# Batch 0 of a fused attention and maxout-MoE kernel in two query parts, with its loads reordered

## Chip, cores, metric

One Trainium2 chip, one core. The metric is the device time of one launch in microseconds, the median of several runs. The profile of the kernel before is of one further run; that of every other kernel is of the first of its runs. PE is TensorE, DVE VectorE, ACT ScalarE, POOL GpSimd, SP SyncE. Every run told here is of the state "fast". Within that state some runs have a mean granted TensorE clock of 0.99 instead of 1.0, and where it matters I give them apart.

## The reference

```python
# q, k, v: (8 batches, 8 heads, 576 rows, 64)
scores = scale * q @ k.T                 # per batch and head
scores = where(block_i >= block_j, scores, -1e9)   # causal in blocks of 64
attn   = exp(scores - max); attn /= attn.sum(-1) + 1e-9
x = (attn @ v)  -> (4608 tokens, 512)
h1, h2 = x @ w1, x @ w2                  # 512 -> 1024
out = maximum(h1, h2) @ w_out            # 1024 -> 512
```

## The kernel before

Heads are handled in pairs (32 pairs, four to a batch; two pairs make a group whose q and k are loaded together). For a pair, PE makes transposed scores (keys on partitions), ACT takes the exp into `aT`, POOL zeroes the half blocks above the diagonal, PE multiplies with V ("AV"; V has a column of ones, so the row sums come along), DVE divides, and PE transposes the result into `xT` ("x_out"), from which the MoE takes 512 tokens at a time ("a span"): h products against w1 and w2, the maximum on DVE, y products against w_out. The MoE's products are dealt out between the attention's by `fill(n)`. q and k are loaded as they are ("plain loads", issued by SP and ACT) and cast to bf16 by an engine; V and the weights are cast on the way ("casting loads", issued by POOL). Feature block f is h's columns 128f to 128f + 127, so block 4 is the first that needs weights from column 512 on, the last to be loaded. The opening of the kernel before:

```python
load_qk(0, (SP, ACT)); load_qk(1, (SP, SP)); load_qk(2, (SP, SP))
# ... casts of groups 0 and 1, V of batch 0, then:
load_w(0, 256); load_w(256, 256)         # on POOL's queue, cast to bf16 on the way

warm_up(16)                              # products of zeros, for the clock
# ... transposes of group 0 ...
for s in range(HP):                      # HP = 4: the pairs of batch 0
    burst_a(s)                           # scores and exps of 1024 + 1024 elements
    # ... casts, transposes, warm_up, av(0, ...) by s ...
    burst_b(s)                           # 1024 + 128
    pool_work(s)                         # s == 0: load_w(512, 512); load_qk(3); s == 3: load_qk(4), V1, w_out
for p in (1, 2, 3):
    av(p, [0, 1]); av(p, [2, 3, 4])      # query tiles of 128 rows
    if p == 2:
        x_out(0)
x_out(1)                                 # only now is a token ready for the MoE
for s in range(HP, NPAIR):               # the even rhythm, with fill() between
    burst_a(s); fill(n_a); burst_b(s); pool_work(s); av(s - 2, ...); ...
```

The softmax here doesn't subtract the row's maximum and nothing guards it: scores larger than these inputs give would overflow.

## Time and profile before

| | before |
|---|---|
| time, median of 4 runs | 294.64 us (293.98 to 294.97) |
| PE busy in the profiled run | 281.2 of 292.3 us |
| of which products of zeros | 36, 10.7 us |
| first useful MoE product | 27.1 us |
| pair 4's first scores (the even rhythm begins) | 32.04 us |
| end of the last product | 289.06 us |

Read it like this: PE is the engine that is full, so the time is PE's list of work plus the stretches in which it does not do useful work.

### The profile page before, as it was taken

The page shows a single profiled execution, that of the slowest core. Times are in us where ns is not written, and L with a number is a line of the kernel's source. Part 1 is how long each engine was busy: PE and PEld are TensorE (multiplying, and loading weights), DVE is VectorE, ACT ScalarE, POOL GpSimd, SP SyncE. Part 2 cuts the span into 40 slices and gives each one's busy share as a digit, 9 for nine tenths or more (in the row PEclk, how much of TensorE's full clock was granted, in tenths as well). Part 3 has the DMA queues.
Part 4 walks back from the last instruction along what each step waited for, and adds up shares of the span by engine and source line. Part 5 has one row for each costly group of instructions (what it writes and reads, how often), then busy time and mean ns, then how long its engine had stood idle before and what let it go on. Part 6 is the DMA issues. An engine that isn't in the chain of part 4 may idle for free.

```text
span 292.3 us, 7455 instructions
## 1 busy us (share of the span) xinstructions
PE 281.2 (96%) x3116; PEld 141.0 (48%) x3116; DVE 181.9 (62%) x363; ACT 140.2 (48%) x200; POOL 95.7 (33%) x236
## 2 busy tenths in 40 slices
PE   8787999999999999999999999999999999999995
PEld 3345445445554454544454455454545544444443
DVE  6717677547986676666565656666665766464530
ACT  3883686686655555554545555545555000101112
POOL 2967536625644443144324532443111000000000
PEclk9999999999999999999999999999999999999999
DMA  7999999968923792568656594465110111011104
GB/s 265 288 182 295 224 183 172 234 150 166 200 34 142 97 212 46 199 73 201 82 200 72 116 168 153 76 61 65 40 38 37 38 69 41 36 72 38 72 36 144
DMA packets 56081, 36.65 MB, mean 125 GB/s; under 512 B 38768, under 2 KB 43376, under 8 KB 56048
## 3 DMA queue, kind: packets, MB, share of 16 engines
q0 software_dynamic: 41728, 7.87, 34.5%
q1 hardware_dynamic: 13760, 27.60, 27.8%
q10 hardware_dynamic: 560, 0.72, 0.7%
q8 instruction: 24, 0.39, 0.6%
q14 instruction: 9, 0.07, 0.1%
HBM read 34.60 MB, written 9.44 MB: 151 GB/s over the span
## 4 chain that ended last, share of the span: by engine, by line
PE 89%; ACT 4%; DVE 3%; DMA 2%; issue 1%; ACTq 0%
PE ps_h L168 43%; PE ps_y L186 20%; PE ps_o L333 11%; PE ps_s L282 8%; ACT aT L288 3%; PE ps_qT L265 2%; DMA qraw<-in_q_dram 2%; PE ps_kT L265 2%; PE ps_xe L353 2%; PE ps_w L254 1%; DVE xp L340 1%; PE ps_y L203 1%; DVE xT L358 0%; DVE qT L272 0%; DVE kT L272 0%
## 5 line engine op out<-in xcount | busy, mean ns | idle before, releaser
L168 PE MATMUL ps_h<-xT,w_sb 128*128 128x512 bf16 x576 | 139.6, 380 | 0.5 <-DVE xT L359 0.4
L288 ACT ACTIVATE aT<-ps_s 128x1024 bf16<-128x1024 f32 (+1 forms) x128 | 99.2, 832 | 53.5 <-PE ps_s L282 53.5
L168 PEld LDWEIGHTS <-w_sb 128*128 128x128 bf16 x576 | 51.8, 98 | 59.7 <-issue 6.1
L175 DVE CAST h<-ps_h 128x512 bf16<-128x512 f32 x72 | 49.7, 691 | 45.0 <-PE ps_h L168 43.9
L186 PE MATMUL ps_y<-wo_sb,g 128*128 128x512 bf16 x280 | 69.6, 379 | 0.0
L293 POOL MEMSET aT<- 64x128 bf16 x128 | 23.6, 200 | 120.7 <-ACT aT L288 120.5
L192 ACT COPY y<-ps_y 128x512 f32<-128x512 f32 x35 | 20.5, 587 | 83.9 <-PE ps_y L186 61.4
L177 DVE TENSOR_TENSOR g<-h,ps_h 128x512 bf16<-128x512 bf16 x72 | 49.3, 684 | 10.2 <-PE ps_h L168 10.2
L333 PEld LDWEIGHTS <-aT 128*128 128x128 bf16 x960 | 33.6, 98 | 14.9 <-DVE xp L340 8.4
L333 PE MATMUL ps_o<-vv,aT 128*128 128x65 bf16 x960 | 39.7, 194 | 0.9 <-DVE xp L340 0.4
L186 PEld LDWEIGHTS <-g 128*128 128x128 bf16 x280 | 25.4, 98 | 27.9 <-issue 3.2
L282 PE MATMUL ps_s<-qT,kT 64*128 64x64 bf16 (+4 forms) x384 | 34.5, 275 | 3.0 <-ACT aT L288 2.9
L109 POOL DMA_DIRECT2D vv<-in_v_dram x40 | 33.7, 848 | 0.3 <-issue 0.3
L340 DVE TENSOR_TENSOR xp<-ps_o,rec 128x256 bf16<-128x256 f32 x64 | 31.4, 491 | 2.2
L282 PEld LDWEIGHTS <-kT 64*128 64x128 bf16 x384 | 16.5, 94 | 18.9 <-issue 13.2
L339 DVE RECIPROCAL rec<-ps_o 128x4 f32<-128x4 f32 x64 | 11.8, 184 | 18.9 <-PE ps_o L333 18.8
L105 POOL CAST qn<-qraw 128x1152 bf16<-128x1152 f32 (+1 forms) x15 | 17.1, 1138 | 4.8 <-DMA qraw<-in_q_dram 4.7
L272 DVE COPY qT<-ps_qT 128x576 bf16<-128x576 bf16 x17 | 12.8, 757 | 5.3 <-PE ps_qT L265 4.1
L358 DVE COPY xT<-ps_xe 128x640 bf16<-128x640 bf16 x16 | 7.8, 490 | 12.4 <-PE ps_xe L353 12.1
L105 POOL CAST kn<-kraw 128x1152 bf16<-128x1152 f32 x13 | 14.9, 1145 | 1.9 <-DMA kraw<-in_k_dram 1.2
L272 DVE COPY kT<-ps_kT 128x576 bf16<-128x576 bf16 x17 | 12.8, 756 | 4.3 <-PE ps_kT L265 3.3
L254 PE MATMUL ps_w<-zeros 128*128 128x512 bf16 x36 | 10.7, 432 | 1.7 <-DVE zeros L132 1.2
(39 smaller groups left out, 102.9 us busy)
## 6 DMA issues: line engine op xcount, KB each, us to landing
qraw<-in_q_dram SPq DMA_DIRECT2D x16, 576.0 KB, 4.4
out_dram<-y SPq DMA_DIRECT2D x35, 256.0 KB, 2.1
kraw<-in_k_dram SPq DMA_DIRECT2D x15, 576.0 KB, 6.5
vv<-in_v_dram POOLq DMA_DIRECT2D x32, 128.0 KB, 5.8
w_sb<-in_moe_w_dram POOLq DMA_DIRECT2D x4, 256.0 KB, 8.1
w_sb<-in_moe_w_dram POOLq DMA_DIRECT2D x2, 512.0 KB, 16.9
wo_sb<-in_moe_w_out_dram POOLq DMA_DIRECT2D x2, 512.0 KB, 12.6
kraw<-in_k_dram ACTq DMA_DIRECT2D x1, 576.0 KB, 5.6
```

Source lines behind the costliest of these rows:

```text
L105: copy(out=n[:, j0:j1], in_=t[:, j0:j1])
L109: nc.gpsimd.dma_start(out=vv_r[b % NV][:rows, c, :, :D], in_=v[b, :, c * P:c * P + rows, :].rearrange("h p d -> p h d"),)
L168: nc.tensor.matmul(pt[:], w_sb[:, c, f * P:(f + 1) * P], xT[:, c, t0:t0 + SPAN], start=(c == 0), stop=(c == NDM - 1),)
L175: nc.vector.tensor_copy(out=h1[:], in_=pt[:])
L177: nc.vector.tensor_max(g[:, f, :], h1[:], pt[:])
L186: nc.tensor.matmul(py[:], g[:, f, s * P:(s + 1) * P], wo_sb[:, f, :], start=(f == 0), stop=(f == NFF - 1),)
L272: copies[i](out=t[:, :S].rearrange("q (p j) -> q p j", j=RPP), in_=pts[i].rearrange("q j p -> q p j"),)
L282: nc.tensor.matmul(ps[:m, hh, col:col + w], kT[r, c * P:c * P + m], qT[r, q0:q0 + w], start=True, stop=True,)
L288: nc.scalar.activation(out=aT_r[p % NA][:m, :, a0:a0 + w], in_=ps[:m, :, :w], func=AF.Exp, scale=scale,)
L293: nc.gpsimd.memset(aT_r[p % NA][BLK:, :, a0:a0 + BLK], 0.0)
L333: nc.tensor.matmul(po[:, gi, hh, :], a[:, hh, a0:a0 + P], vv[:, c, h0 + 2 * hh, :], start=(mm == 0), stop=(mm == n_mm - 1),)
L340: nc.vector.tensor_mul(xp[:, ts[0]:ts[0] + n, :, p % 2], po[:, :, :, :D], rec[:, :n].to_broadcast([P, n, 2, D]),)
```

## The change

The intent: start the MoE earlier. Batch 0 is done in two query parts, queries 0 to 255 of all four pairs first, so that 256 tokens are ready before most of batch 0's exps have run. The MoE's spans become 256, 320, seven of 512 and 448 tokens; a span that does not start on a multiple of 128 carries 64 tokens over (`carry`, copied by POOL). Batch 1's first k load leaves the head of the list and goes behind V0's first tiles, group 4's q and k go behind V1, and the late AV (query tiles 2 to 4) is placed among the later exps. The diff cut to its core (`a_col`, the helpers' width arguments and the plan of MoE units are left out):

```diff
-    NSPAN = NTOK // SPAN
+    spans = [(0, QCUT), (QCUT, S - QCUT)]          # QCUT = 256, S = 576
+    spans += [(t0, min(SPAN, NTOK - t0)) for t0 in range(S, NTOK, SPAN)]
...
-    load_qk(2, (SP, SP))
+    load_qk(2, (SP, None))
-    cast("q", 0, ((dve, 0, 6), (pool, 6, RPP)))
+    cast("q", 0, ((dve, 0, 7), (pool, 7, RPP)))
-    for c in range(3):
+    for c in range(2):
         load_v(0, c)
-    cast("q", 1, ((pool, 0, RPP),))
-    for c in range(3, NCH):
-        load_v(0, c)
-    load_w(0, 256)
-    load_w(256, 256)
+    load_w(0, 256, (0,))
+    cast("k", 1, ((pool, 0, RPP),))
+    load_w(0, 256, (1,))
+    load_qk(2, (None, SP), gated=True)
...
-    warm_up(3)
     cq((0,)); ck((0,)); cq((1,)); ck((1,))          # one line here
-    for s in range(HP): ...                         # the loop above
+    cast("q", 1, ((dve, 0, RPP),))
+    burst_p(0); masks_p(0); burst_p(1); warm_up(2); masks_p(1)
+    for c in range(2, NCH): load_v(0, c)
+    load_w(256, 256)
+    # transposes of group 1 around burst_q1(0)
+    load_w(512, 512)
+    warm_up(3); burst_p(2); av(0, [0, 1]); burst_q3(0); warm_up(2); burst_p(3)
+    masks_p(2, nc.vector); av(1, [0, 1]); masks_p(3, nc.vector); burst_q2(0)
+    av(2, [0, 1]); warm_up(2); burst_q1(1); av(3, [0, 1]); x_out(0, 0, 2); warm_up(2)
+    load_qk(3, (SP, SP), gated=True); cast("q", 2, ((pool, 0, RPP),)); masks_q(0)
+    cast("k", 2, ((pool, 0, RPP),))
+    burst_q2(1); x_out(1, 0, 2); warm_up(2); burst_q3(1); masks_q(1)
+    for c in range(3): load_v(1, c)
+    fill(2); burst_q1(2); av(0, [2, 3, 4]); transposes("q", 2, (dve, act))()
+    burst_q2(2); fill(2); burst_q3(2); masks_q(2)
+    for c in range(3, NCH): load_v(1, c)
+    av(1, [2, 3, 4]); fill(2); burst_q1(3); transposes("k", 2, (dve, act))(); fill(2)
+    x_out(0, 2, NCH); burst_q2(3); av(2, [2, 3, 4]); fill(2); burst_q3(3); masks_q(3)
+    # casts of group 3, load_qk(4), w_out
+    fill(3)
...
     for s in range(HP, NPAIR):
+        burst_a(s)
         if s == HP:
-            # fill(6), transposes of group 2, fill(6)
+            av(3, [2, 3, 4]); fill(5); x_out(1, 2, NCH)
-        burst_a(s)
```

More of the change, by code (lines that the diff above doesn't have):

```diff
@@ L53, with a_col @@
     NCH = 5
-    SPAN = 512
-    NSPAN = NTOK // SPAN
+    QCUT = 256
+    def a_col(p, c, t):
+        if p >= HP:
+            return CB[c] + t * P
+        late = t * P >= QCUT
+        return t * P + {
+            0: 384 - QCUT if late else 0, 1: 704 - QCUT if late else 256 - P,
+            2: 1024 - QCUT, 3: 1408 - 3 * P, 4: 1344 - 4 * P,
+        }[c]
+    SPAN = 512
+    spans = [(0, QCUT), (QCUT, S - QCUT)]
+    spans += [(t0, min(SPAN, NTOK - t0)) for t0 in range(S, NTOK, SPAN)]
+    NSPAN = len(spans)
+    carry = [t0 % P for t0, _ in spans]
+    tiles = [(carry[i] + w) // P for i, (_, w) in enumerate(spans)]
     wpool = ctx.enter_context(tc.tile_pool(name="wpool", bufs=1))
@@ L91, in load_qk @@
         for nm, src, queue in (("q", q, queues[0]), ("k", k, queues[1])):
+            if queue is None:
+                continue
             raws[nm, g] = t = raw.tile([P, 2, RPP * D], FP32, name=f"{nm}raw")
@@ L116, with load_w @@
     wor = moe_w_out.rearrange("(c p) f -> p c f", p=P)
-    def load_w(f0, fw):
-        for dst, src in ((w1_sb, w1r), (w2_sb, w2r)):
+    def load_w(f0, fw, which=(0, 1)):
+        for i in which:
+            dst, src = ((w1_sb, w1r), (w2_sb, w2r))[i]
             nc.gpsimd.dma_start(out=dst[:, :, f0:f0 + fw], in_=src[:, :, f0:f0 + fw])
@@ L160, in h_unit @@
         if f == 0:
-            g_tiles[i] = g_pool.tile([P, NFF, SPAN], BF16, name="g")
+            g_tiles[i] = g_pool.tile([P, NFF, SPAN + BLK], BF16, name="g")
+            if carry[i]:
+                end = carry[i - 1] + spans[i - 1][1]
+                nc.gpsimd.tensor_copy(
+                    out=g_tiles[i][:, :, :carry[i]],
+                    in_=g_tiles[i - 1][:, :, end - carry[i]:end])
         g = g_tiles[i]
-        t0 = i * SPAN
+        t0, w = spans[i]
+        m = carry[i]
         ph = []
@@ L168, in h_unit @@
                 nc.tensor.matmul(
-                    pt[:], w_sb[:, c, f * P:(f + 1) * P], xT[:, c, t0:t0 + SPAN],
+                    pt[:, :w], w_sb[:, c, f * P:(f + 1) * P], xT[:, c, t0:t0 + w],
                     start=(c == 0), stop=(c == NDM - 1),
@@ L174, in h_unit @@
                         h1 = h1_pool.tile([P, SPAN], BF16, name="h1")
-                        nc.vector.tensor_copy(out=h1[:], in_=pt[:])
+                        nc.vector.tensor_copy(out=h1[:, :w], in_=pt[:, :w])
                     else:
-                        nc.vector.tensor_max(g[:, f, :], h1[:], pt[:])
+                        nc.vector.tensor_max(g[:, f, m:m + w], h1[:, :w], pt[:, :w])
                     ph.append(pt)
@@ L182, in y_unit @@
         g = g_tiles[i]
-        t0 = i * SPAN + s * P
+        t0 = spans[i][0] - carry[i] + s * P
         py = ps_m.tile([P, d_model], FP32, name="ps_y", tag="m")
@@ L197, in y_last @@
         g = g_tiles[i]
-        t0 = i * SPAN + s * P
+        t0 = spans[i][0] - carry[i] + s * P
         w = d_model // 2
@@ L214, in y_last, with plan, h, y @@
                 yield
-    def moe():
-        ny = SPAN // P
+    units = []
+    def plan():
+        def h(i, f):
+            t0, w = spans[i]
+            units.append((h_unit(i, f), t0 + w, w / SPAN, 2 * NDM))
+        def y(i, s, last=False):
+            t0, w = spans[i]
+            if last:
+                units.append((y_last(i, s), t0 + w, 0.5, 2 * NFF))
+            else:
+                units.append((y_unit(i, s), t0 + w, 1.0, NFF))
         for i in range(NSPAN):
-            need = (i + 1) * SPAN
             for f in range(NFF):
-                yield from ((need, 0) for _ in h_unit(i, f))
-                if i > 1 and f % 2 == 0:
-                    yield from ((need, 0) for _ in y_unit(i - 1, f // 2))
-            if i == 0:
-                for s in range(ny):
-                    yield from ((need, 0) for _ in y_unit(0, s))
-        for s in range(ny - 1):
-            yield from ((NTOK, 0) for _ in y_unit(NSPAN - 1, s))
-        yield from ((NTOK, 0) for _ in y_last(NSPAN - 1, ny - 1))
-    needs = []
-    for i in range(NSPAN):
-        needs += [(i + 1) * SPAN] * (2 * NDM * NFF + (SPAN // P * NFF if i != 1 else 0))
-    needs += [NTOK] * ((SPAN // P + 1) * NFF)
-    moe_steps = moe()
+                h(i, f)
+                if i > 2 and f % 2 == 0 and f // 2 < tiles[i - 1]:
+                    y(i - 1, f // 2)
+            if i == 1:
+                for j in range(2):
+                    for s in range(tiles[j]):
+                        y(j, s)
+        n = tiles[-1]
+        for s in range(n):
+            y(NSPAN - 1, s, s == n - 1)
+    plan()
+    steps = [(u, need, cost) for u, need, cost, n in units for _ in range(n)]
     at = [0]
     def ready():
-        n = at[0]
-        while n < len(needs) and needs[n] <= done_tokens[0]:
+        n, total = at[0], 0.0
+        while n < len(steps) and steps[n][1] <= done_tokens[0]:
+            total += steps[n][2]
             n += 1
-        return n - at[0]
+        return int(total)
     def fill(n):
-        for _ in range(min(n, ready())):
-            next(moe_steps)
+        while n > 0 and at[0] < len(steps) and steps[at[0]][1] <= done_tokens[0]:
+            u, _, cost = steps[at[0]]
+            next(u)
+            n -= cost
             at[0] += 1
@@ L290, in exp, with mask, burst, burst_p @@
         )
-    def mask(p, a0):
-        nc.gpsimd.memset(aT_r[p % NA][BLK:, :, a0:a0 + BLK], 0.0)
+    def mask(p, a0, eng=None):
+        (eng or nc.gpsimd).memset(aT_r[p % NA][BLK:, :, a0:a0 + BLK], 0.0)
+    def burst(p, parts, a0):
+        u = ps_s.tile([P, 2, 512], FP32, name="ps_s", tag="s")
+        w = 0
+        for c, q0, n in parts:
+            scores(p, u, w, c, q0, n)
+            w += n
+        exp(p, u, w, a0)
+    def burst_p(p):
+        burst(p, ((0, 0, QCUT), (1, P, QCUT - P)), 0)
+    def burst_q1(p):
+        burst(p, ((0, QCUT, 320), (1, QCUT, 192)), 384)
+    def burst_q2(p):
+        burst(p, ((1, 448, P), (2, QCUT, 320), (4, 512, BLK)), 896)
+    def burst_q3(p):
+        burst(p, ((3, 384, 192),), 1408)
+    def masks_p(p, eng=None):
+        for a in (0, 256):
+            mask(p, a, eng)
+    def masks_q(p, eng=None):
+        for a in (1024, 1408):
+            mask(p, a, eng)
     def burst_a(p):
@@ L331, in av @@
                 for c in range(t + 1):
-                    a0 = CB[c] + t * P
+                    a0 = a_col(p, c, t)
                     nc.tensor.matmul(
@@ L343, in av, with x_out @@
         )
-    def x_out(g):
+    def x_out(g, t0=0, t1=NCH):
         b, u = divmod(g, GPB)
-        xp = xps.pop(g)
-        pe = ps_m.tile([P, 2, NCH, BLK], BF16, name="ps_xe", tag="m")
-        po = ps_m.tile([P, 2, NCH - 1, BLK], BF16, name="ps_xo", tag="m")
+        xp = xps[g]
+        n = t1 - t0
+        n_odd = min(t1, NCH - 1) - t0
+        pe = ps_m.tile([P, 2, n, BLK], BF16, name="ps_xe", tag="m")
+        po = ps_m.tile([P, 2, n_odd, BLK], BF16, name="ps_xo", tag="m")
         for s in range(2):
-            for t in range(NCH):
+            for t in range(t0, t1):
                 src = xp[:, t, s].rearrange("p a d -> p (a d)")
-                nc.tensor.transpose(pe[:, s, t, :], src[:BLK], ident[:BLK, :BLK])
+                nc.tensor.transpose(pe[:, s, t - t0, :], src[:BLK], ident[:BLK, :BLK])
                 if t < NCH - 1:
-                    nc.tensor.transpose(po[:, s, t, :], src[BLK:], ident[BLK:, BLK:])
-        dst = xT[:, 2 * u:2 * u + 2, b * S:b * S + NCH * P].rearrange(
+                    nc.tensor.transpose(po[:, s, t - t0, :], src[BLK:], ident[BLK:, BLK:])
+        dst = xT[:, 2 * u:2 * u + 2, b * S + t0 * P:b * S + t1 * P].rearrange(
             "p s (t h w) -> p s t h w", h=2, w=BLK)
         nc.vector.tensor_copy(out=dst[:, :, :, 0], in_=pe[:])
-        nc.vector.tensor_copy(out=dst[:, :, :NCH - 1, 1], in_=po[:])
+        nc.vector.tensor_copy(out=dst[:, :, :n_odd, 1], in_=po[:])
         if u == GPB - 1:
-            done_tokens[0] = (b + 1) * S
+            done_tokens[0] = min(b * S + t1 * P, (b + 1) * S)
     LAG = 2
@@ L376, in pool_work @@
         g, i = divmod(s, 2)
-        if s == 0:
-            load_w(512, 512)
-            load_qk(3, (SP, SP), gated=True)
-        elif s == 1 or s == 2:
-            pass
-        elif s == 3:
-            cast("q", 2, ((act, 0, RPP),))
-            cast("k", 2, ((act, 0, RPP),))
-            load_qk(4, (SP, SP), gated=True)
-            for c in range(3):
-                load_v(1, c)
-            cast("q", 3, ((pool, 0, RPP),))
-            cast("k", 3, ((pool, 0, RPP),))
-            for c in range(3, NCH):
-                load_v(1, c)
-            load_wo(0, 4)
-            load_wo(4, 4)
-        elif s == 4:
+        if s == 4:
             pass
@@ L424 @@
     ck((1,))
-    for s in range(HP):
-        burst_a(s)
-        if s == 0:
-            cast("k", 1, ((dve, 0, RPP),))
-            warm_up(4)
-        elif s == 1:
-            transposes("k", 1, (dve, dve))()
-            warm_up(2)
-        elif s == 2:
-            av(0, [0, 1])
-            warm_up(2)
-        else:
-            av(0, [2, 3, 4])
-        burst_b(s)
-        pool_work(s)
-        if s == 0:
-            transposes("q", 1, (dve, dve))()
-            warm_up(2)
-        elif s == 1:
-            warm_up(4)
-        elif s == 2:
-            warm_up(3)
-    for p in (1, 2, 3):
-        av(p, [0, 1])
-        av(p, [2, 3, 4])
-        if p == 2:
-            x_out(0)
-    x_out(1)
+    cast("q", 1, ((dve, 0, RPP),))
+    burst_p(0)
+    masks_p(0)
+    burst_p(1)
+    warm_up(2)
+    masks_p(1)
+    for c in range(2, NCH):
+        load_v(0, c)
+    load_w(256, 256)
+    cq = transposes("q", 1, (dve, dve))
+    burst_q1(0)
+    ck = transposes("k", 1, (dve, dve))
+    for i in range(2):
+        cq((i,))
+        ck((i,))
+    load_w(512, 512)
+    warm_up(3)
+    burst_p(2)
+    av(0, [0, 1])
+    burst_q3(0)
+    warm_up(2)
+    burst_p(3)
+    masks_p(2, nc.vector)
+    av(1, [0, 1])
+    masks_p(3, nc.vector)
+    burst_q2(0)
+    av(2, [0, 1])
+    warm_up(2)
+    burst_q1(1)
+    av(3, [0, 1])
+    x_out(0, 0, 2)
+    warm_up(2)
+    load_qk(3, (SP, SP), gated=True)
+    cast("q", 2, ((pool, 0, RPP),))
+    masks_q(0)
+    cast("k", 2, ((pool, 0, RPP),))
+    burst_q2(1)
+    x_out(1, 0, 2)
+    warm_up(2)
+    burst_q3(1)
+    masks_q(1)
+    for c in range(3):
+        load_v(1, c)
+    fill(2)
+    burst_q1(2)
+    av(0, [2, 3, 4])
+    transposes("q", 2, (dve, act))()
+    burst_q2(2)
+    fill(2)
+    burst_q3(2)
+    masks_q(2)
+    for c in range(3, NCH):
+        load_v(1, c)
+    av(1, [2, 3, 4])
+    fill(2)
+    burst_q1(3)
+    transposes("k", 2, (dve, act))()
+    fill(2)
+    x_out(0, 2, NCH)
+    burst_q2(3)
+    av(2, [2, 3, 4])
+    fill(2)
+    burst_q3(3)
+    masks_q(3)
+    cast("q", 3, ((pool, 0, RPP),))
+    cast("k", 3, ((pool, 0, RPP),))
+    load_qk(4, (SP, SP), gated=True)
+    load_wo(0, 4)
+    load_wo(4, 4)
+    fill(3)
     x_due = []
@@ L459 @@
         n = fill_of(s)
+        burst_a(s)
         if s == HP:
-            fill(6)
-            cq = transposes("q", 2, (dve, act))
-            ck = transposes("k", 2, (dve, act))
-            cq()
-            ck()
-            fill(6)
-        burst_a(s)
+            av(3, [2, 3, 4])
+            fill(5)
+            x_out(1, 2, NCH)
+            n = fill_of(s)
         n_a = n // 2 if n > 12 else n * 2 // 5
@@ L492 @@
     x_out(NG - 1)
-    fill(len(needs))
+    fill(len(steps))
 _INS = ['q', 'k', 'v', 'moe_w1', 'moe_w2', 'moe_w_out']
```

## The prediction

> **What bounds the kernel now.** I read the page's slices first, then the busy time by stretch, then the chain of waits and the timeline of the opening.
>
> ```profile
> span 292.3 us, 7455 instructions
> PE 281.2 (96%) x3116; PEld 141.0 (48%) x3116; DVE 181.9 (62%) x363; ACT 140.2 (48%) x200; POOL 95.7 (33%) x236
> PE   8787999999999999999999999999999999999995
> ACT  3883686686655555554545555545555000101112
> DMA  7999999968923792568656594465110111011104
> ...
> L254 PE MATMUL ps_w<-zeros 128*128 128x512 bf16 x36 | 10.7, 432 | 1.7 <-DVE zeros L132 1.2
> ```
>
> From the fifth slice on (29 us) PE is full to the last slice: there the time is PE's list of work, and nothing but less work shortens it. Only the opening has slack, and its busy figure flatters it: 36 products of zeros (L254) count as busy.
>
> ```profile
> 20.00:25.00 5.00, 3.96 (x113) 3.43 (x110) 3.54 (x11) 4.54 (x6) 2.62 (x8) 1.00 1.22 277
> 25.00:30.00 5.00, 3.45 (x67) 1.93 (x64) 3.65 (x10) 0.40 (x1) 3.83 (x5) 1.00 1.13 291
> 30.00:35.00 5.00, 4.71 (x61) 2.20 (x61) 3.31 (x6) 2.84 (x5) 2.81 (x6) 1.00 1.62 235
> 35.00:40.00 5.00, 5.00 (x48) 2.25 (x47) 3.76 (x6) 4.25 (x6) 0.75 (x4) 1.00 2.17 162
> ```
>
> Columns: stretch, length, busy us of PE, weight load, DVE, ACT, POOL, clock, DMA share, GB/s. PE fills only at 35 us; ACT all but stops at 25 to 30.
>
> ```profile
> 9.23 1.95 ACT aT L288 x2
> 14.79 0.97 PE ps_w L254 x4
> 19.46 1.95 ACT aT L288 x2
> 24.19 0.56 DVE xp L340
> 28.09 1.02 PE ps_h L168 x4
> 29.60 0.65 ACT qT L272
> 32.11 0.54 PE ps_s L282 x6
> ```
>
> The chain (start, length, what) runs through the exps of batch 0's four pairs one after another (9.2, 12.6, 16.1, 19.5), then through the division by the sums (xp), and reaches the first useful MoE product at 27.1. Pair 4's scores, the start of the even rhythm, are at 32.0; 12 MoE products are done by then.
>
> **What the Trainium skill says.** (1) "TensorE: Matmul & The Clock Gate", section "Wait — 56ns, not 53.3ns?": a warm product takes N/2.4 ns plus about 2.5 ns. The trace agrees: in the chain 16 h products of 512 columns take 3.45 us (216 ns each), the 16 of 256 columns at the end 1.76 us (110). So cutting 512 columns in two costs only some 3 ns. (2) "ScalarE: Activation LUTs", section "What ACT_TABLE_LOAD costs": an ACTIVATE takes 186 ns + 0.833 ns an element, of which about 93 ns overlap with the next; that is 0.95 us per 1024 elements in a row, and the trace has 1.95 us for two. (3) "TensorEngine Tiling (Array Packing)", section "Key Properties": a change of tiling mode drains the array. The trace fits: six 64-row scores, 0.43 us of streaming when the two heads run side by side, hold PE 0.54 us. Interleaving more finely thus costs some 0.1 us a switch. (4) "DMA: Bandwidth & Descriptors", section "Queues, rings and completion order": the DMA engines take turns between queues by packet. Between 22 and 30 us the trace shows just that: 745 packets (1.62 MB) of the plain q/k loads against 763 (0.72 MB) of the casting loads.
>
> **The change part by part.**
>
> *Two query parts.* Queries 0 to 255 of all four pairs are done first, so span 0 of the MoE (256 tokens) can start before most of batch 0's exps have run. By exp, a pair has 768, 1024, 1024 and 384 elements: with 93 + 0.833n ns these are 0.73, 0.95, 0.95, 0.41 us, 3.04 us a pair (measured as 3.00 us with 1024 x3 and 128). So ACT loses nothing much: 12.2 us for the four pairs, 13.5 with the two copies of qT and kT at 0.63 that are now among them.
>
> *When pair 4's scores start.* The zero products between the first transposes and the first scores go (0.81 us on the chain at 8.06); the scores then wait for kT (8.24) and ACT's second qT copy (8.77): first exp at 8.8 instead of 9.2. ACT alone, never waiting, would be through at 8.8 + 13.5 = 22.3. PE's own list from 8.3: 16 score groups about 5.9 us (0.37, 0.42, 0.42, 0.28 a pair), four transposes 1.4, AV 3.0 (0.2 for the first two query tiles, 0.73 for the last three), x_out 0.75, 13 zero products 2.8, fills worth 13 products 2.8: 16.7 us, so 25.0. Neither list runs without waits. I followed both in program order: ACT idles some 0.8 us for q of group 1 (landed 7.9, cast by DVE behind four other DVE jobs until 10.2), 0.5 for kT of pair 2 (four DVE copies of 0.71 after 10.7), up to 1 around the first AV (V0's tiles land at 13 to 14: its data still begins only after the plain loads; before it began at 11 and tile 0 landed at 13.5), and 0.2 to 0.6 at most later bursts, where AV, x_out or a fill stands ahead of the next scores. Sum some 5 us: pair 4's scores at 27 to 28, against 32.0.
>
> *What that is worth.* After that point PE is full in both kernels, so the end moves by the shift, corrected by the work left. Left more: pair 3's AV of three tiles (0.73) and a last x_out, 0.25, with switches 1.1. Left less: 13 instead of 12 units, 0.2. Ten spans instead of nine: 64 more h products at 3 ns, 0.2. Net +1.0 us. DVE gets 16 more copies and maxes for the same columns, and POOL eight carry copies of 64 tokens; both are off the path (62% and 33% busy).
>
> *The loads.* DMA is saturated until 42 us, so the order decides. Rates in the trace: plain loads 0.39 MB/us alone; casting loads 0.155 (V, rows of 128 B) and 0.197 (w) alone; mixed 0.20 and 0.09. Before, the last quarter of the weights (w2, columns 512 up) landed at 35.1. After, g4's q and k no longer go ahead of it: 8 x 0.59 MB / 0.39 = 12.1, V0 0.59 / 0.155 = 3.8, w 2.1 / 0.197 = 10.7, from a start at 2.6: 29.2, plus 1 to landing, so 30 to 31. PE wants it at the 36th product of 256 columns (h feature block 4): from the start of pair 4's scores 0.5 for them, 0.8 for AV, 1.1 for ten such products, 0.25 for x_out, so 2.7 us later: 30 to 31. It is just in time; if the attention part ran faster than I think, this load would hold it back. w_out then lands near 42, first needed near 47: hidden.
>
> Sum: 294.7 - (32.0 - 28.0) + 1.0 = 291.7; with 27.5, 291.2. I take 291.4.
>
> **The rivals.** (a) *The weights bound it*: the opening runs at ACT's or PE's bare list (25) but w2 comes at 31 or later. For it: DMA nine tenths busy throughout, and k of group 2 and g3 cut into the same engines. Against: in the kernel before no product waited for w. Then 292 to 293. (b) *In-order queues eat the gain*: POOL issues ten casting loads of 0.7 to 1.0 us between 12 and 25 and the masks stand behind them, while DVE is some 85% busy by my count (casts, eight T copies, divisions, h). A wait of 1 to 2 us in PE's order gives 293 to 295. For it: POOL's and DVE's lists; against: the late AV is placed where masks of query part two should be set (POOL at 19.3, PE at 19.5). (c) *The opening packs perfectly*: 25 and weights on time give 288.7. PE's list is a floor, so more than 2% (below 288.8) is at the very edge.
>
> **Range and chances.** Working shifts of 2 to 6.5 us, less 1.0, give 289.2 to 293.7 us, which I take at 8 in 10. Faster by over 2%: 0.09. Within 2%: 0.88. Slower by over 2%: 0.03, if a wait of the new order goes deep.
>
> **What would show it.** First h product near 18.3 instead of 27.1; first exp at 8.8; pair 4's scores at 27 to 28 (the step that carries the number); zero products 29 instead of 36 (16 + 13); h products 640; PE full from there to the end, with the same 216 ns rhythm. Wrong if: the chain in the opening shows a weight or V landing, or POOL's masks, for over 1 us; if pair 4's scores come before 26 or after 30; or if the even stage itself changes its length (new gaps from the carry copies or the half-width maxes), which I count as none.

## The result, and the profile after

292.08 us, median of 4 runs (291.84 to 292.33), against 294.64 of the kernel before in the same series. The ratio is 0.9916, 95% interval 0.9896 to 0.9936. Ratios here are the mean time of one kernel's runs over that of the other's of the same rounds, so not quite the ratio of the medians quoted. Within 2%, and inside the predicted range; 0.7 us above the predicted 291.4.

The page of the kernel after, for the lines shown of before: span, busy times, and PE's row of slices (tenths, 40 slices).

```profile
span 290.0 us, 7655 instructions
...
PE 281.0 (97%) x3189; PEld 146.0 (50%) x3189; DVE 184.8 (64%) x387; ACT 138.6 (48%) x198; POOL 101.7 (35%) x243
...
PE   8799999999999999999999999999999999999995
```

PE's first eight slices are fuller; its total of busy time has hardly moved (281.2 to 281.0), since seven products of zeros went and h became finer. The busy time by stretch, in the columns of the prediction:

```profile
20.00:25.00 5.00, 4.55 (x103) 3.26 (x103) 3.60 (x9) 3.19 (x6) 4.77 (x10) 1.00 1.20 272
25.00:30.00 5.00, 5.00 (x91) 3.79 (x90) 3.08 (x10) 3.75 (x5) 2.76 (x5) 1.00 1.37 234
30.00:35.00 5.00, 4.43 (x65) 3.35 (x62) 4.34 (x12) 1.51 (x4) 2.29 (x9) 1.00 2.26 164
...
50.00:55.00 5.00, 4.37 (x69) 2.11 (x67) 3.15 (x8) 3.32 (x5) 3.44 (x7) 1.00 0.87 244
```

The stretches 20 to 25 and 25 to 30 now have 4.55 and 5.00 us of PE instead of 3.96 and 3.45. But 30 to 35 has 4.43, less than before (4.71), and 50 to 60 is not full either (nor was it before). PE's own order of time shows the steps (start, length, what, count; in brackets what PE sat idle for just before):

```profile
18.12 0.61 PE L196 MATMUL ps_h<-xT,w_sb 128*128 128x256 bf16 x4
...
19.88 0.43 PE L402 MATMUL ps_o<-vv,aT 128*128 128x65 bf16 x9 [0.44 <-DMA vv<-in_v_dram]
20.58 0.34 PE L402 MATMUL ps_o<-vv,aT 128*128 128x65 bf16 x6 [0.27 <-DMA vv<-in_v_dram]
...
27.69 0.61 PE L323 MATMUL ps_s<-qT,kT 64*128 64x512 bf16 x6
...
31.25 1.70 PE L196 MATMUL ps_h<-xT,w_sb 128*128 128x256 bf16 x14 [0.57 <-DMA w_sb<-in_moe_w_dram]
```

The first h product is at 18.12, pair 4's scores (64x512) at 27.69. There are two waits for loads: AV of pair 0 for V0's last tiles, until 20.58, and the h products of feature block 4 for w2's last half, until 31.25. (Of the 0.57 us shown there, the last load accounts for 0.37: where w2 is in time, as in five kernels below, PE still idles 0.20 at this place, for DVE.) The chain that ended last, over the first 45 us (start, length, what):

```profile
1.75 7.39 DMA kraw<-in_k_dram
...
11.82 2.40 POOL vv L131 x3
...
16.41 14.79 DMA w_sb<-in_moe_w_dram
...
31.25 1.70 PE ps_h L196 x14
```

Before, this part of the chain was exps and divisions. Now it is the k load of group 1, POOL's cast and POOL's issuing of loads, and then 14.79 us of one load, the last half of w2. The page's shares of the whole chain say the same, DMA having gone from 2% to 8%:

```profile
PE 86%; DMA 8%; POOL 2%; ACT 1%; DVE 1%; issue 1%; SPq 0%; ACTq 0%; POOLq 0%
```

Where the gain went can be counted from two more stretches, from pair 4's scores to the end of the last product, of before and of after:

```profile
32.04:289.06 257.02, 255.81 (x2757) 127.55 (x2756) 162.13 (x310) 121.15 (x174) 73.79 (x189) 1.00 0.56 108
```

```profile
27.69:286.80 259.11, 257.07 (x2841) 133.16 (x2840) 164.54 (x326) 121.16 (x174) 82.14 (x203) 1.00 0.57 112
```

The start of this stretch moved by 32.04 - 27.69 = 4.35 us, its end only by 289.06 - 286.80 = 2.26. So 2.09 us were given back: PE's busy time in it grew by 257.07 - 255.81 = 1.26, its idle time from 1.21 to 2.04, by 0.83 (0.57 just before block 4, 0.16 from there to 45 us, 0.10 later).

### The profile page after: what moved, and what is told of

Same layout as the page of the kernel before. It is cut to its first block, busy times and chain, and to the rows that moved or that the text cites. A ratio compares the mean times of both kernels' runs of the same rounds, so it can differ in the third digit from the quotient of the medians.

```text
span 290.0 us, 7655 instructions
## 1 busy us (share of the span) xinstructions
PE 281.0 (97%) x3189; PEld 146.0 (50%) x3189; DVE 184.8 (64%) x387; ACT 138.6 (48%) x198; POOL 101.7 (35%) x243
## 4 chain that ended last, share of the span: by engine, by line
PE 86%; DMA 8%; POOL 2%; ACT 1%; DVE 1%; issue 1%; SPq 0%; ACTq 0%; POOLq 0%
PE ps_h L196 42%; PE ps_y L214 20%; PE ps_o L402 11%; PE ps_s L323 7%; DMA w_sb<-in_moe_w_dram 5%; DMA kraw<-in_k_dram 3%; PE ps_xe L424 2%; PE ps_qT L306 2%; PE ps_kT L306 2%; POOL w_sb L143 1%; POOL vv L131 1%; ACT aT L329 1%; PE ps_y L231 1%; POOL kn L127 0%; SPq L117 0%
## 5 line engine op out<-in xcount | busy, mean ns | idle before, releaser
L196 PE MATMUL ps_h<-xT,w_sb 128*128 128x512 bf16 (+3 forms) x640 | 140.5, 358 | 0.7 <-DMA w_sb<-in_moe_w_dram 0.6
L329 ACT ACTIVATE aT<-ps_s 128x1024 bf16<-128x1024 f32 (+3 forms) x128 | 100.0, 832 | 58.5 <-PE ps_s L323 56.1
L196 PEld LDWEIGHTS <-w_sb 128*128 128x128 bf16 x640 | 57.7, 98 | 56.4 <-issue 5.7
L203 DVE CAST h<-ps_h 128x512 bf16<-128x512 f32 (+3 forms) x80 | 50.9, 637 | 44.4 <-PE ps_h L196 42.2
L205 DVE TENSOR_TENSOR g<-h,ps_h 128x512 bf16<-128x512 bf16 (+3 forms) x80 | 50.5, 632 | 9.2 <-PE ps_h L196 7.2
L323 PE MATMUL ps_s<-qT,kT 64*128 64x64 bf16 (+6 forms) x400 | 35.0, 271 | 1.6 <-ACT kT L313 0.7
L409 DVE TENSOR_TENSOR xp<-ps_o,rec 128x256 bf16<-128x256 f32 (+1 forms) x64 | 31.4, 491 | 2.2
L408 DVE RECIPROCAL rec<-ps_o 128x4 f32<-128x4 f32 (+1 forms) x64 | 11.8, 185 | 17.1 <-PE ps_o L402 17.0
L186 POOL COPY g<-g 128x512 bf16<-128x512 bf16 x8 | 4.9, 613 | 37.9 <-DVE g L205 37.8
L429 DVE COPY xT<-ps_xe 128x640 bf16<-128x640 bf16 (+2 forms) x18 | 8.1, 453 | 12.5 <-PE ps_xe L424 12.0
```

Source lines behind the costliest of these rows:

```text
L196: nc.tensor.matmul(pt[:, :w], w_sb[:, c, f * P:(f + 1) * P], xT[:, c, t0:t0 + w], start=(c == 0), stop=(c == NDM - 1),)
L203: nc.vector.tensor_copy(out=h1[:, :w], in_=pt[:, :w])
L205: nc.vector.tensor_max(g[:, f, m:m + w], h1[:, :w], pt[:, :w])
L323: nc.tensor.matmul(ps[:m, hh, col:col + w], kT[r, c * P:c * P + m], qT[r, q0:q0 + w], start=True, stop=True,)
L329: nc.scalar.activation(out=aT_r[p % NA][:m, :, a0:a0 + w], in_=ps[:m, :, :w], func=AF.Exp, scale=scale,)
L409: nc.vector.tensor_mul(xp[:, ts[0]:ts[0] + n, :, p % 2], po[:, :, :, :D], rec[:, :n].to_broadcast([P, n, 2, D]),)
```

## The experiments

Twelve kernels ran, each correct, in three series of four on three chips; each series has its own runs of the kernel before (medians 294.10, 294.02 and 294.21 us). All but two start from the kernel after. "Full clock" means a mean granted clock of at least 0.998. The last columns are from each kernel's profile: pair 4's first scores, and the start of the 14 h products of feature block 4, which need w2's last part (in `w_quarter`, `pad4`, `k2_early`, `w_384` and `combo` PE's idle time before it is put down to DVE, not to w2; for the last two kernels it was not read). In the profiled run of `old_loads`, the slowest of its six (297.73), and in that of `spans_only` the clock was low.

| kernel | median us | ratio to before | full-clock runs, mean | lower clock, mean | pair 4 | block 4 |
|---|---|---|---|---|---|---|
| after, with the result | 292.08 | 0.9916 | 4, 292.08 | 0 | 27.69 | 31.25 |
| after_again | 292.81 | 0.9961 | 3, 292.13 | 3, 293.55 | 28.21 | 31.66 |
| w_quarter | 293.25 | 0.9983 | 4, 293.18 | 2, 295.05 | 29.27 | 32.46 |
| pad4 | 293.67 | 0.9978 | 3, 292.69 | 3, 294.62 | 28.67 | 31.86 |
| k2_early | 293.01 | 0.9943 | 2, 291.74 | 4, 293.07 | 27.88 | 31.07 |
| old_loads | 295.56 | 1.0032 | 0 | 6, 295.67 | 27.84 | 34.27 |
| w_384 | 292.31 | 0.9941 | 6, 292.34 | 0 | 28.31 | 31.50 |
| no_zeros | 293.07 | 0.9965 | 0 | 6, 293.05 | 28.21 | 31.55 |
| late_av_behind | 292.41 | 0.9951 | 5, 292.27 | 1, 294.50 | 26.91 | 30.93 |
| v0_first | 291.85 | 0.9932 | 5, 291.80 | 1, 293.94 | 26.90 | 31.10 |
| combo | 291.40 | 0.9924 | 5, 291.44 | 1, 294.16 | 27.13 | 30.32 |
| spans_only | 295.65 | 1.0050 | 5, 295.55 | 1, 295.92 | 33.09 | - |
| loads_only | 294.48 | 1.0011 | 6, 294.46 | 0 | 32.48 | - |

The last two columns, with the landings in the traces, account for the spans. In the ten profiles with the query parts that have full clock from block 4 on (all of them but `old_loads`), the span is block 4's start plus 258.7 to 258.8 us (259.0 in `combo`, whose block 4 itself takes 0.28 us longer): what stands behind that point took the same time in all of them. And block 4 starts 3.19 us after pair 4's scores where no weight is late (five kernels), or else some 0.05 us after w2's last half has landed (`after` and `after_again`, `old_loads`, `no_zeros`, `late_av_behind`, `v0_first`). In the seven kernels other than `old_loads` that load columns 512 up in one piece, that landing lies between 30.8 and 31.6 us.

My theory at the start: w2's landing near 31.2 is what the sum of the prediction lacked. Rivals: PE's and the other engines' in-order lists; the clock.

**The changed kernel again.**

> The changed kernel itself once more, to stand beside the others on the same chip, and to see whether it too has runs with a mean granted clock of 0.994 (four of six runs of the kernel with batch 1's k early had it, and were 1.3 us longer). Theory: 292.0 where the clock is 1.0; if some runs show 0.994, they are some 1.4 us longer.

Both happened. Three runs at full clock have a mean of 292.13, three at 0.993 or 0.994 one of 293.55, 1.4 us more. None of the 33 runs of the kernel before in the three series has a clock below 0.998. So the gain of the change is 0.7 to 0.8% at full clock (0.9916 in the first series, 0.9932 here), and 0.4% in this series as it fell. Where in the kernel the clock drops in those three runs is open: the profiled runs of the changed kernel were all at full clock. By size (an estimate from these spans), a mean of 0.994 over 291 us is some 3.5 us at half clock; the profile of `spans_only`, at 0.994, shows one such stretch, from 28.0 to 31.6 us.

**Four products of zeros more.**

```diff
     fill(3)
+    warm_up(4)
```

> Four more products of zeros (4 x 0.216 = 0.87 us of PE) just ahead of pair 4's scores. Theory: PE runs into the wait for w2 at 31.2 whatever stands before it, so the wait swallows about 0.6 us of the 0.87 and the time rises by 0.2 to 0.3 us, to about 292.3. Rival (PE's list is what counts, the wait is an artefact of the record): the full 0.87 us, 293.0.

```profile
28.67 0.61 PE L323 MATMUL ps_s<-qT,kT 64*128 64x512 bf16 x6
...
31.86 1.69 PE L196 MATMUL ps_h<-xT,w_sb 128*128 128x256 bf16 x14 [0.20 <-DVE g L205]
```

Pair 4's scores came 0.98 us later than in the profile of the result, the products on w2's last half only 0.61 us later (31.86 against 31.25), and the span grew by 0.6 (290.0 to 290.6). So the wait swallowed 0.37 us, less than the 0.6 that I expected: the theory's mechanism holds, its size does not. Of the 0.57 us of the first profile, 0.20 stay, since they are DVE's: in this profile w2 had landed at 30.9, and the 0.20 before 31.86 are put down to DVE. Full-clock runs: 292.69 against 292.08 to 292.13.

**The old order of loads.**

```diff
-    load_qk(2, (SP, None))
+    load_qk(2, (SP, SP))
-    load_qk(2, (None, SP), gated=True)
     ...
     masks_q(1)
+    load_qk(4, (SP, SP), gated=True)
     for c in range(3):
         load_v(1, c)
     ...
-    load_qk(4, (SP, SP), gated=True)
     load_wo(0, 4)
```

> The query parts with the old order of loads: batch 1's k at the head, and q and k of group 4 ahead of V1 as before. Theory (DMA is saturated and w2 the next bound): group 4's 1.18 MB cost w2's last half 3 us, it lands at 34 and PE waits 3 to 4 us: 294.5 to 295.5, the gain gone. Rival (order of loads doesn't matter, the attention chain decides): 292.1 to 292.6.

The gain is gone: 295.56, with all six runs at 0.988 to 0.994. The profile is of the slowest run, the one at 0.988; the other five took 294.33 to 296.32. PE's order of time at block 4, and two stretches around it (the third figure from the end is the clock):

```profile
34.27 3.17 PE L195 MATMUL ps_h<-xT,w_sb 128*128 128x256 bf16 x14 [3.44 <-DMA w_sb<-in_moe_w_dram]
```

```profile
32.00:34.00 2.00, 0.00 (x0) 0.00 (x0) 0.00 (x0) 0.00 (x0) 0.14 (x1) 0.82 1.80 222
34.00:36.00 2.00, 1.73 (x9) 1.24 (x10) 0.42 (x1) 0.00 (x0) 0.00 (x0) 0.50 2.39 160
```

Pair 4's scores are where they were (27.84), so the attention part of the change works with the old loads too. But w2's last half lands at 34.2, as expected, PE stands still for 3.44 us, and then the clock falls to 0.50: the 14 products that took 1.70 us now take 3.17. How much of the loss is the wait and how much the clock, these runs don't separate. The load order is therefore not a side matter; without it the two query parts gain nothing.

**Only batch 1's k early.**

```diff
-    load_qk(2, (SP, None))
+    load_qk(2, (SP, SP))
-    load_qk(2, (None, SP), gated=True)
```

> Only batch 1's first k load goes back to the head of the list, as in the kernel before. V0's first two tiles should land some 1.5 us later (13.3 and 14.3 instead of 11.8 and 12.8), the first AV waits for them at 12.95, pair 4's scores move by up to 1.3 us; w2's last half still lands at 31, since the same bytes are ahead of it, so the wait for it swallows 0.6. Theory: plus 0.3 to 0.8 us, about 292.6. Rival (this reordering is the heart of the gain): plus 1.5 us or more.

V0's first two tiles landed at 13.1 and 14.1, nearly as expected, but V0's last tile at 20.72 (20.54 in the result's profile), so pair 4's scores moved only by 0.2 us; w2's last half landed at 30.8, and the two full-clock runs have a mean of 291.74, no slower than the changed kernel. Four of the six runs are at 0.994, with 293.07. So of the two parts of the load order it is group 4's q and k that matter (they are what `old_loads` has besides, with w2 landing 3.4 us later); this one moves no time at full clock. Whether it makes the low clock more frequent, six runs can't say.

**The weights in smaller pieces.** Two kernels.

```diff
-    load_w(512, 512)
+    load_w(512, 256)
+    load_w(768, 256)
```

> The last half of w1 and w2 (feature columns 512 up) is loaded in four quarters (w1 512-767, w2 512-767, then the two of 768 up) instead of two halves, so w2's columns for feature block 4 should land about 2.6 us earlier (28.6 instead of 31.2). Theory (the wait for w2 at 31.25 holds PE some 0.6 to 0.7 us and is what the sum of the prediction lacked): 0.5 to 0.8 us less than the changed kernel, about 291.4, pair 4's scores still at 27.7, no wait on w_sb. Rival (in-order queues eat it: POOL's two more load issues of 0.75 us push the masks back, or DVE is the holder): 292.1 or more.

The rival was right, through a wait that I had not thought of. POOL's order of time, and an entry of the waits between 6 and 45 us (who waited for whom: total, times, longest):

```profile
19.33 0.74 POOL L143 DMA_DIRECT2D w_sb<-in_moe_w_dram  x1 [1.60 <-DMA vv<-in_v_dram]
```

```profile
PE ps_o L402 <- POOL aT L334: 2.4, 1, 2.4
```

POOL's last weight load could not be issued until a V load had landed, with eight casting loads under way. The limit is the program's own: in the trace POOL's loads take eight completion semaphores (108 to 115) in turn, and this load waits for 112, which V0's third tile holds until it lands at 19.05. The 1.6 us hold POOL's masks back, AV of pair 0 waits 2.4 us for them, and pair 4's scores are at 29.27. No wait for w2 is left, and the kernel is 1.1 us slower all the same (293.18 at full clock).

```diff
-    load_w(256, 256)
+    load_w(256, 384)
...
-    load_w(512, 512)
+    load_w(640, 384)
```

> The weights' second and third loads are cut at feature column 640 instead of 512 (384 + 384 instead of 256 + 512 columns of w1 and w2), so the number of POOL's load issues stays at four and feature block 4 comes with the middle pair: its w2 should land at about 26 instead of 31.2. Theory (the wait for w2 holds PE 0.4 us, from 30.86 to 31.25; the last 0.2 before it is x_out waiting for DVE): span 0.3 to 0.5 us less at clock 1.0, 289.6, time about 291.6, no wait on w_sb. Rival: same as the changed kernel to 0.1 us, because another wait takes its place.

```profile
27.55 0.83 PE L196 MATMUL ps_h<-xT,w_sb 128*128 128x256 bf16 x6 [0.36 <-DMA w_sb<-in_moe_w_dram]
```

Same as the changed kernel (292.34 at full clock, against 292.13 on the same chip): the middle pair, now larger, landed later, and PE waited for it 0.36 us before pair 4's scores instead of after. The rival's case: a wait took the place of another. (0.2 us between such means is less than the spread of one kernel's full-clock runs, 291.69 to 292.40 in `after_again`.)

**Without the zeros.** All six `warm_up` calls after pair 0's first scores go, 13 products.

```diff
-    warm_up(2)      (five places)
-    warm_up(3)      (one place)
```

> The 13 products of zeros after pair 0's first scores are dropped (2.8 us of PE). Theory (PE's own list in the opening is close to its length, but w2 at 31.2 bounds it): pair 4's scores 0.5 to 2 us earlier, all swallowed by the wait for w2, so span within 0.3 us of the changed kernel where the clock stays 1.0. Second thing it tells: if the zeros are there for the clock, runs at 0.99 or lower appear and cost 1.3 us or more. Rival (PE's list decides): 2 us or more faster.

PE's order of time, two places:

```profile
20.83 0.61 PE L402 MATMUL ps_o<-vv,aT 128*128 128x65 bf16 x15 [0.55 <-DMA vv<-in_v_dram]
```

```profile
28.21 0.61 PE L323 MATMUL ps_s<-qT,kT 64*128 64x512 bf16 x6
```

With 2.8 us of PE work less, pair 4's scores are at 28.21, to the hundredth where the changed kernel has them on the same chip. AV of pair 0 waits for V0 until 20.83 (in `after_again` until 21.10, for its last six products), both kernels go on to the transposes of q at 21.37, and everything behind falls in line. So V0's last tile holds both. But this run is no clean test of PE's list, because the clock changed with it, by stretches of a microsecond (PE busy comes after the length, the clock is the third figure from the end):

```profile
9.00:10.00 1.00, 0.10 (x4) 0.00 (x0) 0.95 (x1) 1.00 (x2) 0.95 (x1) 1.00 1.39 311
...
11.00:12.00 1.00, 0.05 (x2) 0.05 (x4) 1.00 (x3) 0.72 (x1) 0.95 (x5) 0.91 1.77 161
12.00:13.00 1.00, 0.95 (x10) 0.47 (x10) 1.00 (x2) 0.50 (x1) 1.00 (x2) 0.50 1.50 192
```

From 11.9 to 18.5 PE runs at half clock, so its products take twice as long. That took back what the missing zeros gave: PE comes to the late AV of pair 0 at 18.88, in `after_again` at 18.92. In this profile it cost no time in the end, since in both kernels PE then waits for V0. Three of the six runs (0.988) have a mean of 292.21, those at 0.981 and 0.982 one of 293.89.

**V0's last tiles ahead of w2's first quarter.**

```diff
-    load_w(0, 256, (1,))
     load_qk(2, (None, SP), gated=True)
     ...
     for c in range(2, NCH):
         load_v(0, c)
+    load_w(0, 256, (1,))
     load_w(256, 256)
```

> V0's last three tiles are issued ahead of w2's first quarter. Theory (the opening hangs on two landings: V0's last tile near 20.6 sets pair 4's scores 7.1 us later, w2's last half at 31.2 sets the rest): V0's last tile lands 1 us or more earlier, the wait of AV for it goes, pair 4's scores at 26.9 to 27.4 instead of 27.7 to 28.2, and the wait for w2 grows by as much: span 289.7 to 290.4, no change in time. Rival (V0 is the only bound): 0.7 us or more faster.

```profile
19.23 0.90 PE L401 MATMUL ps_o<-vv,aT 128*128 128x65 bf16 x24
...
26.90 0.61 PE L322 MATMUL ps_s<-qT,kT 64*128 64x512 bf16 x6
...
31.10 1.70 PE L195 MATMUL ps_h<-xT,w_sb 128*128 128x256 bf16 x14 [1.21 <-DMA w_sb<-in_moe_w_dram]
```

As the theory has it, step by step: AV of pair 0 at 19.23 with no wait, pair 4's scores at 26.90, and the time thus won goes into a wait of 1.21 us for w2. ACT tells the same. Its idle time before its second qT copy, in the result's profile and here:

```profile
21.41 0.64 ACT L313 COPY qT<-ps_qT 128x576 bf16<-128x576 bf16 x1 [1.29 <-PE ps_qT L306]
```

```profile
20.62 0.64 ACT L312 COPY qT<-ps_qT 128x576 bf16<-128x576 bf16 x1 [0.26 <-PE ps_qT L305]
```

Its six other waits from the first exp to pair 4's scores are the same to 0.01 us in the two profiles, so the 1.03 us are the whole difference; with a first exp 0.23 us later (9.49 against 9.26) the scores win 0.79. Full-clock runs 291.80, against 292.08 and 292.13 on other chips. As ratios to the kernel before of their own series (mean of full-clock runs over mean of the runs of before) that is 0.9919 against 0.9916 and 0.9932: no change.

**The late AV behind the exps.** The three `av(p, [2, 3, 4])` of pairs 0 to 2 and `x_out(0, 2, NCH)` move behind `masks_q(3)`.

```diff
-    av(0, [2, 3, 4])    (from among the bursts of batch 0's second part,
-    av(1, [2, 3, 4])     one place each)
-    x_out(0, 2, NCH)
-    av(2, [2, 3, 4])
     ...
     masks_q(3)
+    av(0, [2, 3, 4])
+    av(1, [2, 3, 4])
+    av(2, [2, 3, 4])
+    x_out(0, 2, NCH)
```

> The late AV (query tiles 2 to 4) of pairs 0 to 2 stands behind the last exp of batch 0 instead of among the exps. Theory: the same PE list in another order; the AV of pair 0 no longer stands in wait for V0's last tiles (0.7 us), the exps run with less idle, and the AVs are paid at the end: pair 4's scores at 26.5 to 28, w2 still at 31, so 291.8 to 292.4. Rival (the spreading is what makes the opening short): 293.5 or more.

```profile
26.91 0.61 PE L323 MATMUL ps_s<-qT,kT 64*128 64x512 bf16 x6
...
30.93 1.70 PE L196 MATMUL ps_h<-xT,w_sb 128*128 128x256 bf16 x14 [1.04 <-DMA w_sb<-in_moe_w_dram]
```

Pair 4's scores come at 26.91, earlier than with the AV spread: nothing stands waiting for V0 (and the first exp came at 8.62 instead of 9.26); then w2 holds PE for 1.04 us. 292.27 at full clock: the spreading of the late AV, by itself, is worth nothing here.

**Parts alone, on the kernel before.** `loads_only`: the kernel before with batch 1's k behind V0's first tiles and w's first quarter, and group 4's q and k behind V1. `spans_only`: the kernel before, its opening and loads untouched, with the ten spans (the changed kernel's plan and fillers). The first, on the kernel before:

```diff
-    load_qk(2, (SP, SP))
+    load_qk(2, (SP, None))
     ...
-    for c in range(3):
+    for c in range(2):
         load_v(0, c)
+    load_w(0, 256, (0,))
     cast("q", 1, ((pool, 0, RPP),))
-    for c in range(3, NCH):
+    load_w(0, 256, (1,))
+    load_qk(2, (None, SP), gated=True)
+    for c in range(2, NCH):
         load_v(0, c)
-    load_w(0, 256)
     ...
-            load_qk(4, (SP, SP), gated=True)   (now behind V1's loads)
```

> The kernel before with only the loads reordered: batch 1's k behind V0's first tiles and w's first quarter, group 4's q and k behind V1. Theory: nothing in the kernel before waits for these loads in the opening (its chain is exps and divisions), so no change within 0.5 us: 293.7 to 294.7. Rival (the loads bring the gain): 293 or less.

294.48, 1.0011 times the kernel before: nothing, as expected.

> The kernel before with its own attention opening and its own loads, but the MoE in ten spans (256, 320, seven of 512, 448) instead of nine. Theory: the list grows by 64 products at 3 ns and some switches, 0.2 to 0.4 us; and since feature block 4 now comes after 16 units of work instead of 32, PE meets w2's last half (35.1 in the kernel before) and may wait up to 1 us: 294.5 to 295.5. Rival (the spans alone bring the gain): 293 or less.

295.65, 1.0050 times. The direction and size are as expected, but not by the wait that I gave for it: no wait for w2 shows, and the profiled run (at 0.994) had w2's last half at 33.9, before PE came to it. From pair 4's scores to the end of the span it has 260.8 us, against 260.2 of the kernel before, so some 0.6 us comes after that point, with the longer list. The rest of the 1.4 us I can't place: this profile's pair 4 comes 1.05 us later than the kernel before's (33.09), with a clock of 0.80 and 0.86 in the two stretches from 25 to 35 us, but the other five runs were at full clock and slow as well.

**A combination.** The late AV behind the exps, the weights cut at column 640, and:

```diff
-    load_qk(3, (SP, SP), gated=True)
     cast("q", 2, ((pool, 0, RPP),))
     ...
     masks_q(1)
+    load_qk(3, (SP, SP), gated=True)
     for c in range(3):
         load_v(1, c)
```

> Three edits at once for a better kernel: late AV of pairs 0 to 2 behind the exps (pair 4's scores 1.3 us earlier when it ran alone), weights cut at column 640, q and k of group 3 issued after the masks of pair 1 (some 3 us later, so that w2 has the DMA engines first). Theory: both landings out of the way, so the earlier scores reach the end: span 288.7 to 289.4 at clock 1.0, time 290.7 to 291.4. Rival (the engines move the same bytes, some load of the opening still holds PE): 291.7 or more, with a wait on w_sb or on q and k of group 3.

```profile
27.13 0.61 PE L323 MATMUL ps_s<-qT,kT 64*128 64x512 bf16 x6
...
30.32 1.98 PE L196 MATMUL ps_h<-xT,w_sb 128*128 128x256 bf16 x14 [0.20 <-DVE g L205]
```

291.40, and 291.44 at full clock: the best kernel, 0.9924 of the kernel before with all its runs, 0.9906 with the full-clock ones, which the changed kernel has at 0.9916 and 0.9932. Before block 4 PE idles 0.2 us, for DVE, and within its 14 products (1.98 us instead of 1.70) a weight load waits 0.4 us for w; pair 4's scores (27.13) and block 4 (30.32) are both early. The difference from the changed kernel, some 0.6 us, was not measured on one chip side by side, so it is likely rather than shown.

## Why the prediction was right, point by point

*The range and the mechanism.* Right. The opening had the slack, the MoE's start moved to 18.12 (18.3 predicted), zero products fell to 29 and h products rose to 640, as said.

*Pair 4's scores at 27 to 28.* Right (27.69; 28.21 in the other series), and on the whole for the reason given: ACT's list with its idle time. The prediction had a start at 8.8, 13.5 us of work and some 5 us of idle time; in the profile ACT starts the exps at 9.26, idles 4.2 us in seven waits, and is through at 27.5. That the late start and the shorter idle time nearly cancel is luck. One wait stands elsewhere than predicted: V0's first tiles, given up to 1 us, landed before they were wanted (11.8 and 12.7, with AV at 12.95); it was V0's last tile (20.5), which the prediction did not weigh, that cost 1.03 of the 4.2 us. `v0_first` shows it: with that tile 1.05 us earlier the scores come at 26.90.

*The first exp at 8.8.* It was at 9.26, as in the kernel before (9.23), so nothing was gained there. The 16 products of zeros at the start ran until 7.5 instead of 6.4, and the transposes of q, which stand behind them in PE's order, began at 7.45 instead of 6.60. In other profiles of the same opening they begin at 6.80 to 7.69, and the first exp comes at 8.60 to 9.49; why they differ, no run tells.

*w2 lands at 30 to 31, just in time.* Nearly right as a computation (31.2; with 1.18 MB more ahead of it 34.2, where the sum gives 3.0 us more), and this is rival (a) in a small dose. The term of the sum that was missing is the idle time before block 4, 0.57 us, of which w2 accounts for 0.37. PE's side was too short as well: block 4 comes 3.19 us after pair 4's scores where nothing is late, not 2.7. `v0_first` and `late_av_behind` show the landing as a floor: what the opening wins, it loses there, and `combo`, which no longer needs the last load for block 4, starts it at 30.32.

*What would show it wrong.* One of the signs came, by the letter: a weight's landing stands in the chain for 14.79 us, where I had set 1 us. PE's own wait for it was 0.57 us at most, so the sign, as I worded it, said more than the wait cost. The time, 292.08, fits rival (a)'s 292 to 293 too; what tells them apart is the opening, which took until 27.7 and not 25.

*Net +1.0 us of work left.* Its own terms add up to +1.1 (1.1 - 0.2 + 0.2). Measured as +1.26 us of busy time. The ten spans were probably the undersized piece: 0.2 predicted, some 0.6 seen after pair 4's scores in `spans_only`.

*PE full from there on.* Wrong in both kernels: between 45 and 65 us PE idles 1.1 us before and 1.2 after. It is nearly the same, so it does not enter the difference.

*The sum.* 294.7 - 4.35 + 1.26 + 0.83 gives 292.4, against 292.08 measured; with the spans of the two profiles it is exact (292.3 - 290.0 = 2.3, and 2.26 by the end of the last product).

*Rival (b), the in-order queues.* Not in the changed kernel, but `w_quarter` shows that it was two load issues away: the ninth casting load under way has to wait.

*What I did not think of.* That the changed kernel is liable to a lower clock: in its second series three of six runs had it, at 1.4 us each, in the first none of four. What brings it on stays open.

## What to carry to other kernels

When work is moved forward in a kernel's opening, list the landings that it will meet there, with the time each is needed and the bytes ahead of it; here the order of the loads decided whether 4 us of earlier start became 2.5 us of time or none. An engine's list is only a bound if taking work off it moves something: drop some work that does not matter and look, but see that the clock stayed the same. And cutting a load into smaller pieces adds issues to an engine's queue, where the program's limit on loads under way can hold back quite other work.

## What the Trainium skill lacked or had wrong

- "TensorE: Matmul & The Clock Gate", the table of section "Why this matters for your kernels": it asks for no idle gap over about 3 us. That suffices as a warning for `old_loads` (a wait of 3.44 us, then clock 0.50), but not as a rule: in `no_zeros` no wait of PE between 7 and 12 us was longer than 1.03 us, PE was busy 2.14 us of those 5 (3.34 in the kernel after, which kept its clock), and the clock still went to 0.50 from 11.9 to 18.5 us. Four groups of transposes, 0.43 to 0.44 us each, are most of the 2.14; whether they count as work for the clock, no run here separates.
- The same page, section "Back-to-back issue gap": it gives about 131 ns a product of 512 columns as the sustained rate with weight loads. In the chain of the kernel before 16 h products, each with its weight load, take 3.45 us, 216 ns each, which is what the page's other formula, N/2.4 + 2.5, says.
- "DMA: Bandwidth & Descriptors", section "Specifications" and section "Queues, rings and completion order": about 1 us to the first byte of a load issued by POOL, and turns between the queues by packet. V0's first tile was issued at 6.15 us in the kernel after and at 6.85 in the kernel before; its first packets moved between 9 and 10 us, and between 10 and 11, when the plain loads were running out. From 22 to 30 us of the kernel before the turns by packet are there (745 packets of plain loads against 763 of casting loads). Whether the late start is a start-up time or the plain loads' precedence, no run here tells.
